# Attention values product in column halves, and block means from the loaded values: a change to a fused attention and two-MLP kernel

## The chip, the cores and the metric

The kernel runs on one core of a Trainium2 chip. The metric is the device time of one execution in microseconds (us), the median of several runs. The engines are TensorE (PE; its weight loads are shown apart as PEld), VectorE (DVE), ScalarE (ACT), GpSimd (POOL) and SyncE (SP), whose queue issues the DMA transfers here.

## The reference, cut to what matters

Two batches, 8 heads, 768 positions, head width 64, all float32. Each query attends to the keys less than 16 positions away and to 24 block summaries (block of 32 positions): the summary key is the block's maximum, the summary value its mean. The result goes through a gated MLP with an RMS norm and a second MLP.

```python
k_sum = k.reshape(B, H, nb, block, D).max(axis=3)
v_sum = v.reshape(B, H, nb, block, D).mean(axis=3)
scores_l_m = np.where(mask_l, scale * np.matmul(q, k.T), -1e9)
scores_s = scale * np.einsum('bhsd,bhnd->bhsn', q, k_sum) + np.log(block)
a = softmax(concatenate([scores_l_m, scores_s]))
v_all = np.concatenate([v, v_sum], axis=2)
x = np.matmul(a, v_all)                 # (1536, 512) after the heads are joined
xn = x / rms(x) * rms_g
x = (silu(xn @ w_gate) * (xn @ w_val)) @ w_out      # 512 -> 1536 -> 512
out = (s * relu(x @ w_in) ** 2 + b) @ w_out2        # 512 -> 2048 -> 512
```

## The kernel before

The 1536 rows (2 batches of 768) are 12 tiles of 128 queries. A tile is two halves of 64 queries; each half has its own window of 96 keys and the 24 summaries, so 120 keys in all (`KW` = 96, `KC` = 120). Heads go in two groups of four, so there are 24 groups of (tile, four heads).

For each group: `do_qk` (L587) multiplies queries and keys, four float32 matmuls; `do_top` (L597, DVE) adds the mask and finds the row maximum; `do_exp` (L604, ACT) takes the exponential and its sum; `do_t` (L615, PE) transposes the probabilities; `do_pt` (L634, ACT) copies the transposes out of PSUM; `do_pv` (L643, PE) is the values product; `do_norm` (L652, DVE) divides by the sum. A float32 matmul of the program shows as two MATMUL records in the trace.

The values product before: for each head one matmul, stationary the 120x128 transposed probabilities, moving the values of both halves beside one another (2 x 64 columns). All 128 queries are multiplied with the values of both windows, so half of what lands in PSUM is not wanted. `do_norm` is called twice for a group, once for each half: 64 partitions x 256 elements each.

The values lie in SBUF as slots of 96 window rows x 512 columns, one for each half tile (`vslot`), loaded by `load_v` (L282, six transfers of 384 KB for a batch). The 24 means stand in rows 96 to 119 of each slot. Before the change the means come from a second, transposed copy of v: `load_vt` (L322 and L327, four transfers of 384 KB for a batch, those of batch 1 into the ring of weight buffers `raw`), `sum_vt` (L332, one DVE reduction for each), `turn_vs` (L339, ACT, two small copies), `mean_vt` (L345, two PE transposes), `put_v` (L352 on DVE, L354 on ACT, scaling by 1/32 into a slot), and `spread_v` (L357), which copies the means by DMA from the slots that have them to the others.

From the six tiles on, the MLPs follow. Their weights are split in a high and a low part (DVE, ACT, POOL), and products run as float32r matmuls of 128x512 (L789, L790, L793, then L912, L913, L915). The first chunks of the first MLP (`HEAD` = 3, for three groups of 512 rows) are mixed with the attention as fill.

The order of the work up to there is made by a planner written out in the kernel: `plan` makes tasks with an engine, a cost, dependencies and a rank, and `give_out` (L373) issues, on a modelled clock, on each engine the task of lowest rank that could start. The result is a fixed program order for each engine, and each engine works through it in order. When TensorE would be idle in the plan, `give_out` issues four transposes of the identity matrix (L459), whose result nothing uses. SP's queue, too, is in a fixed order, and an issue that must wait holds those behind it.

Of the kernel before, what the change touches and what calls it, by code (L numbers as in the profile page):

```python
# [30 lines left out]
GH = 4  # L31
# [25 lines left out]
@with_exitstack  # L57
def kernel(ctx: ExitStack, tc: tile.TileContext, q_t, k_t, v_w, v_t, w_gate, w_val, w_out, w_in2, w_out2, rms_g, s2, b2, out):
    nc = tc.nc
# [41 lines left out]
    def bank(i):  # L101
        return psp.tile([128, 512], F32, tag=f"b{i}", name=f"b{i}")
# [9 lines left out]
    junk = const.tile([128, DM], mybir.dt.bfloat16, name="junk")  # L112
    qz = [const.tile([128, 2, GH, 128], F32, name=f"qz{i}") for i in range(2)]
    part = const.tile([128, NSUB * 4 * SUB], F32, name="part")

# [14 lines left out]
    def vslot(b, s):  # L130
        return vst[b][s // NTL][:, s % NTL]
# [18 lines left out]
    def consts_mask2():  # L150
        m, far = masks[1], masks[0]
        nc.gpsimd.tensor_copy(m[64:128, 0:KW], far[64:128, 0:KW])
        nc.gpsimd.memset(m[:, KW:KC], math.log(BLK) / scale)
        for i, p0, o in ((0, 0, HQ), (2, 64, HQ + WIN)):
            nc.gpsimd.tensor_copy(masks[i], m)
            nc.gpsimd.memset(masks[i][p0:p0 + 64, o:o + WIN], NEG / scale)

    def load_small():
# [149 lines left out]
    mean_ps = {}  # L308
    vt_t = {}
    vs_t = {}  # L310

    def vs_of(b):
        if b == 0:
            return vt0[:, NPAIR * SEQ:NPAIR * SEQ + 512]
        if b not in vs_t:
            vs_t[b] = tmp("vs")
        return vs_t[b]

    def load_vt(b, pr):
        if b == 0:  # L320
            t = vt_t[b, pr] = vt0[:, pr * SEQ:(pr + 1) * SEQ]
            nc.sync.dma_start(out=t, in_=v_t[b, pr])  # L322
            return
        t = rawp.tile([128, 512, 2], I32, tag="raw", name="vt")
        t = t.rearrange("p f c -> p (f c)")[:, 0:SEQ]
        vt_t[b, pr] = t.bitcast(F32)
        nc.sync.dma_start(out=t, in_=v_t[b, pr].bitcast(I32))  # L327

    def sum_vt(b, pr):

        c0 = pr * 128 + KW
        nc.vector.tensor_reduce(out=vs_of(b)[:, c0:c0 + NS].rearrange("p (c e t) -> p t c e", c=2, e=2),  # L332
                                in_=vt_t.pop((b, pr)).rearrange("p (t c e i) -> p t c e i", c=2, e=2, i=BLK), axis=AX.X, op=ALU.add)

    def turn_vs(b, pairs):

        vs = vs_of(b).rearrange("p (a c) -> p a c", a=NPAIR)[:, pairs]
        for o, a in ((64, KW + 12), (76, KW)):
            nc.scalar.activation(out=vs[:, :, o:o + 12], in_=vs[:, :, a:a + 12], func=AF.Copy)  # L339

    def mean_vt(b, pairs, i):
        vs = vs_of(b).rearrange("p (a c) -> p a c", a=NPAIR)[:, pairs]
        ps = mean_ps[b, pairs.start] = bank(i)
        for j in range(pairs.stop - pairs.start):
            nc.tensor.transpose(ps[:, j * 128:(j + 1) * 128], vs[:, j], ident)  # L345

    def put_v(b, s, pairs, eng):
        p0 = 64 if s % 2 else KW
        o = vslot(b, s)[KW:KC, pairs.start * 128:pairs.stop * 128]
        a = mean_ps[b, pairs.start][p0:p0 + NS, 0:(pairs.stop - pairs.start) * 128]  # L350
        if eng == "DVE":
            nc.vector.tensor_scalar(out=o, in0=a, scalar1=1.0 / BLK, scalar2=None, op0=ALU.mult)  # L352
        else:
            nc.scalar.activation(out=o, in_=a, func=AF.Copy, scale=1.0 / BLK)  # L354
# [116 lines left out]
    def mb(b):  # L471
        return b / 0.31e6

    def plan(x):
# [3 lines left out]
        cm2 = task("POOL", 1.4, consts_mask2, [cm], rank=-29.5)  # L478
        K, Q, V, VT, KM, VM = {}, {}, {}, {}, {}, {}

# [14 lines left out]

        def lvt(b, pr, rank):
            VT[b, pr] = task("SP", mb(128 * 768 * 4), lambda: load_vt(b, pr), rank=rank, take=("raw",) if b else ())

        def lv(b, t, rank):
# [6 lines left out]
        lq(1, (-6, -2.8))  # L506
        lvt(0, 0, -5)
        lvt(0, 1, -4.5)
        lv(0, 0, -4.2)
        lk(0, 4, -4)  # L510
        lk(0, 6, -3)
        lvt(0, 2, -2)
        lvt(0, 3, -1)
        for t in range(1, NTL):
            lv(0, t, t - 1.5)
        sml = task("SP", mb(128 * 516 * 4), load_small, rank=1.2)
        for h in range(0, NH, 2):
            lk(1, h, 4 + 0.5 * h)
        for pr in range(NPAIR):
            lvt(1, pr, 5.5 + pr)  # L520
        for t in range(NTL):
            lv(1, t, 9 + t)

# [19 lines left out]
        def means(b, rank):  # L543
            z = task("POOL", pl(512) / 3, lambda: nc.gpsimd.memset(vs_of(b), 0.0), rank=rank - 2 if b else -28)
            for g in range(2):
                pairs = slice(2 * g, 2 * g + 2)
                sums = [task("DVE", dve(768), lambda pr=pr: sum_vt(b, pr), [VT[b, pr], z], rank + 1.5 * g,
                             give=(("raw", VT[b, pr]),) if b else ()) for pr in (2 * g, 2 * g + 1)]
                tv = task("ACT", 0.54, lambda pairs=pairs: turn_vs(b, pairs), sums, rank + 1.5 * g)
                tr = task("PE", 0.22, lambda i, pairs=pairs: mean_vt(b, pairs, i), [tv, ci], rank + 1.5 * g, bank="M")  # L550
                VM[b, g] = tr
                puts = []
                for s in range(4 if b == 0 else 2):
                    e = ("ACT", "DVE")[s % 2]
                    puts.append(task(e, act(256) if e == "ACT" else dve(256), lambda s=s, e=e, pairs=pairs: put_v(b, s, pairs, e),
                                     [tr, *puts[-1:]] if s < 3 else [tr, puts[-1]], rank + 1.5 * g + s // 2))
                puts[-1]["free"] = (tr,)
                VM[b, g, "put"] = puts
            for t in range(NTL):
                if b == 0 and t < 2:  # L560
                    VM[b, t, "ok"] = [VM[b, g, "put"][2 * t + k] for g in range(2) for k in range(2)]
                elif b and t == 0:
                    VM[b, t, "ok"] = [p for g in range(2) for p in VM[b, g, "put"]]
                else:
                    first = [p for g in range(2) for p in VM[b, g, "put"]]
                    VM[b, t, "ok"] = [task("SP", 0.3, lambda s=s: spread_v(b, s), first, 2 * (6 * b + t) - 6) for s in (2 * t, 2 * t + 1)]
        means(0, -3.0)
# [8 lines left out]
        for n, (i, g) in enumerate(us):  # L576
# [60 lines left out]
            def do_pv(bk, i=i, g=g, b=b, t=t):  # L637
# [3 lines left out]
                for j in range(GH):  # L641
                    h = GH * g + j
                    nc.tensor.matmul(X[:, j * 128:(j + 1) * 128].rearrange("p (c d) -> p c d", c=2), PT[0:KC, j * 128:(j + 1) * 128],  # L643
                                     vv[:, :, h * HD:(h + 1) * HD], start=True, stop=True)
            C = pv[i, g] = task("PE", 0.88, do_pv, [pt, V[b, t], *VM[b, t, "ok"]], n + 0.2, bank="X", give=(("PT", pt),))

            def do_norm(c, i=i, g=g):
                if i not in X_of:
                    X_of[i] = xnp.tile([128, DM], F32, tag="xn", name="xn")
                p = slice(64 * c, 64 * c + 64)  # L650
                xv = box["X", i, g].rearrange("p (h c d) -> p h c d", h=GH, c=2)
                nc.vector.tensor_tensor(out=X_of[i][p, g * GH * HD:(g + 1) * GH * HD].rearrange("p (h d) -> p h d", h=GH),  # L652
                                        in0=xv[p, :, c],
                                        in1=sm_of[i][p, 1, GH * g:GH * g + GH].rearrange("p (h o) -> p h o", o=1).broadcast_to([64, GH, HD]),
                                        op=ALU.mult)
            N = [task("DVE", dve(256), lambda c=c, f=do_norm: f(c), [C, rc], n + 0.0) for c in range(2)]
            N[1]["deps"].append(N[0])
            N[1]["free"] = (C,)
            if g:
                N[0]["deps"].append(box["N", i][1])  # L660
                A["deps"].append(qk[i, 0])
# [6 lines left out]
            N = N + box["N", i]  # L668
            N[1]["give"] = (("sm", box["A0", i]),)

# [20 lines left out]
            if i == TPS:  # L691
                deps += [VM[0, 0], VM[0, 1]]
            if i == 2 * TPS:
# [249 lines left out]
def _layout(q, k, v, moe_w_gate, moe_w_val, moe_w_out, moe_rms_g, moe2_w_in, moe2_w_out, moe2_s, moe2_b):  # L943
# [26 lines left out]
    def strips(w):  # L970
# [5 lines left out]
        "v_w": c(vw),  # L976
        "v_t": c(v.reshape(NB, NPAIR, 2, SEQ, HD).transpose(0, 1, 2, 4, 3)).reshape(NB, NPAIR, 128, SEQ),
        "w_gate": c(strips(moe_w_gate)).reshape(KF, 128, 512),
# [30 lines left out]
```

## Time and profile before

| | us |
|---|---|
| median of 3 runs | 658.63 (654.58 to 660.88) |
| span of the profiled execution | 658.8 |
| PE busy in it | 634.1 (96%) |
| DVE busy | 396.6 (60%) |
| ACT busy | 269.8 (41%) |
| POOL busy | 153.8 (23%) |

The profile shows one execution. Busy time of PE is modelled, since matmuls are pipelined: where it is below the length of a stretch, TensorE waited at least that long. The span runs from the first to the last instruction; the page gives nothing of what lies around it, so 658.8 us is taken as this execution's own time.

### The profile page before, as it was taken

What the parts mean: (1) busy time and instruction counts of PE and PEld (TensorE: products, weight loads), DVE (VectorE), ACT (ScalarE), POOL (GpSimd) and SP (SyncE); (2) the same over time, 40 slices, a digit from 0 to 9 for tenths busy, and PEclk for the clock granted to TensorE, in tenths of its full rate; (3) what the DMA queues carried; (4) which work ended last, traced back from release to release, by engine and by line L of the source; (5) the groups of instructions that cost most, each with busy time, mean ns of one, the idle gap of its engine ahead of it and who ended that gap; (6) DMA issues with size and microseconds to landing.
All of it is one profiled execution on the core that took longest, in us unless ns stands there. A gap on an engine that the chain in (4) does not pass through costs nothing.

```text
span 658.8 us, 8381 instructions
## 1 busy us (share of the span) xinstructions
PE 634.1 (96%) x3052; PEld 529.9 (80%) x3052; DVE 396.6 (60%) x778; ACT 269.8 (41%) x615; POOL 153.8 (23%) x187
## 2 busy tenths in 40 slices
PE   4878989999999999999999999999999999999998
PEld 3777778888888888888888888888888888888886
DVE  5769999524681455554555666881278647855632
ACT  3765878332453333311333325552455035404400
POOL 3345756340331111111111111110221022102100
PEclk9989999999999999999999999999999999999999
DMA  9989951100342111111211111122021301120022
GB/s 290 266 248 269 276 160 66 33 0 14 115 135 89 59 66 67 64 66 64 65 64 65 64 60 42 61 66 93 1 96 65 97 32 65 64 65 0 1 96 97
DMA packets 20929, 59.36 MB, mean 90 GB/s; under 512 B 2664, under 2 KB 2920, under 8 KB 20888
## 3 DMA queue, kind: packets, MB, share of 16 engines
q1 hardware_dynamic: 20888, 58.83, 28.6%
q8 instruction: 24, 0.39, 0.3%
q14 instruction: 17, 0.14, 0.1%
HBM read 54.79 MB, written 3.15 MB: 88 GB/s over the span
## 4 chain that ended last, share of the span: by engine, by line
PE 86%; DVE 5%; DMA 4%; ACT 2%; SPq 1%; issue 1%; POOL 0%; DVEq 0%; ACTq 0%; POOLq 0%
PE b L793 21%; PE b L789 21%; PE b L790 21%; PE b L913 7%; PE b L915 7%; PE b L912 7%; DMA qz<-in_q_t_dram 3%; PE b L587 1%; ACT P L604 1%; SPq L357 1%; DMA hg<-in_k_t_dram 1%; PE b L643 1%; DVE ks L292 1%; DVE xn L652 1%; DVE wa L219 1%
## 5 line engine op out<-in xcount | busy, mean ns | idle before, releaser
L235 POOL TENSOR_TENSOR wl<-wa,wh 128x512 fp32r<-128x512 f32 x68 | 89.5, 1323 | 388.2 <-ACT wh L231 315.0
L789 PE MATMUL b<-x,wh 128*128 128x512 f32 x288 | 113.5, 394 | 0.3
L790 PE MATMUL b<-x,wl 128*128 128x512 f32 x288 | 112.3, 390 | 0.4 <-POOL wl L235 0.4
L231 ACT ACTIVATE wh<-wa 128x512 fp32r<-128x512 f32 x68 | 41.5, 626 | 98.8 <-PE b L915 45.5
L793 PE MATMUL b<-x,wh 128*128 128x512 f32 x288 | 77.6, 391 | 0.0
L913 PE MATMUL b<-wl,hg 128*128 128x512 f32 (+1 forms) x196 | 75.1, 385 | 0.0
L912 PE MATMUL b<-wh,hg 128*128 128x512 f32 (+1 forms) x196 | 75.1, 385 | 0.0
L789 PE MATMUL b<-y,wh 128*128 128x512 f32 x192 | 74.7, 389 | 0.0
L790 PE MATMUL b<-y,wl 128*128 128x512 f32 x192 | 74.7, 389 | 0.0
L894 DVE SCALAR_TENSOR_TENSOR b<-u,sbc 128x512 f32<-128x512 f32 x48 | 50.7, 1056 | 35.6 <-ACT u L893 35.6
L790 PEld LDWEIGHTS b<-x,wl 128*128 128x128 f32 x288 | 54.1, 188 | 11.4 <-POOL wl L235 0.7
L789 PEld LDWEIGHTS b<-x,wh 128*128 128x128 f32 x288 | 54.2, 188 | 11.3 <-issue 0.7
L793 PEld LDWEIGHTS b<-x,wh 128*128 128x128 f32 x288 | 53.6, 188 | 10.8
L789 PE MATMUL b<-hg,wh 128*128 128x512 f32 x144 | 56.0, 389 | 0.0
L790 PE MATMUL b<-hg,wl 128*128 128x512 f32 x144 | 56.0, 389 | 0.0
L814 DVE SCALAR_TENSOR_TENSOR hg<-b,bbc,hg 128x512 fp32r<-128x512 f32 x48 | 36.0, 749 | 28.2 <-ACT hg L813 28.2
L220 DVE SCALAR_TENSOR_TENSOR wa<-raw,wa 128x512 int32<-128x512 int32 x68 | 50.5, 743 | 2.1
L915 PE MATMUL b<-wh,hg 128*128 128x512 f32 (+1 forms) x196 | 51.5, 385 | 0.0
L793 PE MATMUL b<-y,wh 128*128 128x512 f32 x192 | 51.3, 389 | 0.0
L219 DVE SCALAR_TENSOR_TENSOR wa<-raw,wa 128x512 int32<-128x512 int32 x68 | 49.9, 734 | 2.1
L813 ACT ACTIVATE hg<-b,bbc 128x512 fp32r<-128x512 f32 x48 | 33.0, 687 | 42.9 <-DVE b L894 42.9
L921 DVE TENSOR_TENSOR part<-b,part 128x512 f32<-128x512 f32 (+1 forms) x37 | 24.4, 673 | 43.4 <-PE b L915 43.4
(94 smaller groups left out, 1010.3 us busy)
## 6 DMA issues: line engine op xcount, KB each, us to landing
raw<-in_w_out_dram SPq DMA_DIRECT2D x28, 512.0 KB
raw<-in_w_in_dram SPq DMA_DIRECT2D x16, 512.0 KB
qz<-in_q_t_dram SPq DMA_DIRECT2D x24, 256.0 KB
raw<-in_w_gate_dram SPq DMA_DIRECT2D x12, 512.0 KB
raw<-in_w_val_dram SPq DMA_DIRECT2D x12, 512.0 KB
vt<-in_v_t_dram SPq DMA_DIRECT2D x8, 384.0 KB
hg<-in_k_t_dram SPq DMA_DIRECT2D x5, 576.0 KB
out_dram<-part SPq DMA_DIRECT2D x11, 256.0 KB
```

Source lines behind the costliest of these rows:

```text
L219: lambda: nc.vector.scalar_tensor_tensor(out=ai, in0=hi, scalar=-0x80000000, in1=ai, op0=ALU.bitwise_and, op1=ALU.bitwise_or),
L220: lambda: nc.vector.scalar_tensor_tensor(out=ai, in0=lo, scalar=29, in1=ai, op0=ALU.logical_shift_right, op1=ALU.bitwise_or),
L231: nc.scalar.activation(out=r(h), in_=a_t[i], func=AF.Copy)
L235: nc.gpsimd.tensor_tensor(out=r(lo), in0=a_t.pop(i), in1=high[i], op=ALU.subtract)
L789: nc.tensor.matmul(ps, r(hi[:, kk * 128:(kk + 1) * 128]), xh, start=kk == 0, stop=False)
L790: nc.tensor.matmul(ps, r(lo[:, kk * 128:(kk + 1) * 128]), xh, start=False, stop=False)
L793: nc.tensor.matmul(ps, r(hi[:, kk * 128:(kk + 1) * 128]), r(act(kk, 1)), start=False, stop=kk == 3)
L814: nc.vector.scalar_tensor_tensor(out=r(dst[1]), in0=ps, scalar=bias, in1=dst[0], op0=ALU.add, op1=ALU.subtract)
L894: after(0, lambda u=u, ps=ps: nc.vector.scalar_tensor_tensor(out=ps, in0=u, scalar=sbc[:, 0:1], in1=u, op0=ALU.mult, op1=ALU.mult))
L912: nc.tensor.matmul(acc, gh, r(ws[e][0][:, cs]), start=e == 0, stop=False)
L913: nc.tensor.matmul(acc, gh, r(ws[e][1][:, cs]), start=False, stop=False)
L915: nc.tensor.matmul(acc, r(ge[e][:, 1]), r(ws[e][0][:, cs]), start=False, stop=e == 3)
```

## The change

The values product is made in two column halves: for each head two matmuls, one for each half of 64 queries, with 64 stationary columns and 64 moving columns, writing PSUM partitions 0 to 63 and 64 to 127. All 256 columns that land are wanted, and one `do_norm` of 128 partitions x 256 serves the group.

The block means are made from the loaded value slots. `sel` is a selection matrix of 0 and 1: `add_v` makes, for each of a batch's 12 slots, one float32 matmul of 64x32 by 64x512, which adds the two blocks of the slot into two of 32 PSUM rows; slots go by turns to the four strips of 32 partitions. `sums_v` copies the PSUM bank out (ACT), `mean_v` adds the four strips with one matmul (`comb`), and `put_v` writes 24x512 into a slot. The transposed copy of v is neither made on the host nor loaded. Ranks of the loads change: the six value loads of batch 0 come ahead of the queries of tile 2. The DMA scratch is made smaller.

```diff
+    def consts_sel():                      # POOL, 3 memsets
+        nc.gpsimd.memset(sel[0:64], 0.0)
+        nc.gpsimd.memset(sel[0:32, 17:18], 1.0)
+        nc.gpsimd.memset(sel[32:64, 23:24], 1.0)
+    def consts_comb():                     # POOL, 1 memset and 12 copies
+        nc.gpsimd.memset(comb, 0.0)
+        for j in range(4):
+            p = slice(32 * j, 32 * j + 32)
+            for o, a, n in ((KW, 0, 24), (64, 12, 12), (76, 0, 12)):
+                nc.gpsimd.tensor_copy(comb[p, o:o + n], ident[p, 32 * j + a:32 * j + a + n])
-    def load_vt(b, pr): ...
-    def sum_vt(b, pr): ...
-    def turn_vs(b, pairs): ...
-    def mean_vt(b, pairs, i): ...
+    def add_v(b, a, i):
+        if a == 0:
+            mean_ps[b] = bank(i)
+        for s in range(4 * a, 4 * a + 4):
+            j = s % 4
+            n0 = 12 * (s % 2) + s // 2
+            nc.tensor.matmul(mean_ps[b][32 * j:32 * j + 32], sel[0:64, 17 - n0:49 - n0], vslot(b, s)[0:64], start=a == 0, stop=a == 2)
+    def sums_v(b):
+        nc.scalar.activation(out=vs_of(b), in_=mean_ps[b], func=AF.Copy)
+    def mean_v(b, i):
+        ps = mean_ps[b] = bank(i)
+        nc.tensor.matmul(ps[0:KC], comb[:, 0:KC], vs_of(b), start=True, stop=True)
-    def put_v(b, s, pairs, eng):           # 24 x 256
+    def put_v(b, s, eng):                  # 24 x 512
-        lvt(0, 0, -5)
-        lvt(0, 1, -4.5)
-        lv(0, 0, -4.2)
+        lv(0, 0, -5)
+        lv(0, 1, -4.5)
-        lvt(0, 2, -2)
-        lvt(0, 3, -1)
-        for t in range(1, NTL):
-            lv(0, t, t - 1.5)
+        for t in range(2, NTL):
+            lv(0, t, -2.7 + 0.1 * t)
-        for pr in range(NPAIR):
-            lvt(1, pr, 5.5 + pr)
         for t in range(NTL):
-            lv(1, t, 9 + t)
+            lv(1, t, 6 + 0.6 * t)
+            for a in range(3):
+                add.append(task("PE", 0.9, lambda *i, a=a: add_v(b, a, *i or (None,)), [V[b, 2 * a], V[b, 2 * a + 1], cs, *add[-1:]],
+                                rank, bank="M" if a == 0 else None))
+            cp = task("ACT", act(512), lambda: sums_v(b), add[2:], rank, free=(add[0],))
+            tr = task("PE", 0.88, lambda i: mean_v(b, i), [cp, cc], rank, bank="M")
-                    nc.tensor.matmul(X[:, j * 128:(j + 1) * 128].rearrange("p (c d) -> p c d", c=2), PT[0:KC, j * 128:(j + 1) * 128],
-                                     vv[:, :, h * HD:(h + 1) * HD], start=True, stop=True)
+                    for c in range(2):
+                        nc.tensor.matmul(X[64 * c:64 * c + 64, j * HD:(j + 1) * HD], PT[0:KC, j * 128 + 64 * c:j * 128 + 64 * c + 64],
+                                         vv[:, c, h * HD:(h + 1) * HD], start=True, stop=True)
-            N = [task("DVE", dve(256), lambda c=c, f=do_norm: f(c), [C, rc], n + 0.0) for c in range(2)]
+            N = [task("DVE", dve(256), do_norm, [C, rc], n + 0.0, free=(C,))]
```

## Rows read from the trace of the kernel before

**Rows 1.** Busy time of each engine in four stretches: us, busy (instructions), clock, DMA share, GB/s

```profile
20.00:36.00 16.00, 11.46 (x94) 10.39 (x93) 10.39 (x47) 11.42 (x47) 6.61 (x13) 1.00 0.92 213
36.00:84.00 48.00, 44.08 (x305) 38.69 (x305) 42.57 (x150) 35.36 (x127) 27.64 (x43) 0.96 0.93 274
84.00:96.00 12.00, 9.34 (x82) 8.88 (x80) 11.66 (x25) 8.61 (x23) 7.86 (x8) 1.00 0.47 135
96.00:122.00 26.00, 24.98 (x165) 21.57 (x164) 24.59 (x79) 20.27 (x72) 14.61 (x23) 1.00 0.26 90
```

**Rows 2.** Chain of work that ended last: start us, us, what

```profile
15.43 9.68 DMA qz<-in_q_t_dram
25.17 10.46 DMA qz<-in_q_t_dram
...
47.78 0.42 DVE xn L652
...
57.22 0.86 DVE vs L332
...
72.23 0.43 DVE xn L652
...
80.97 0.88 DVE vs L332
...
92.00 3.35 DMA raw<-in_w_val_dram
...
101.01 0.89 PE b L643 x8
```

**Rows 3.** Timeline of the DMA issues on SP's queue, 80 to 95 us

```profile
83.80 8.09 SPq L357 DMA_DIRECT2D part<-part  x10
```

**Rows 4.** DMA view of the first 36 us: packets, bytes, mean rate; an issue group

```profile
DMA packets 4327, 9.37 MB, mean 260 GB/s; under 512 B 757, under 2 KB 757, under 8 KB 4323
...
vt<-in_v_t_dram SPq DMA_DIRECT2D x4, 384.0 KB
```

**Rows 5.** DVE groups by line, 0 to 122 us: busy us, mean ns

```profile
L652 DVE TENSOR_TENSOR xn<-b,sm 64x256 f32<-64x256 f32 x48 | 20.1, 419 | 2.1 <-PE b L643 0.9 <-POOL ss L679 0.3
...
L704 DVE TENSOR_TENSOR x<-b,x 128x512 fp32r<-128x512 f32 x11 | 7.5, 686 | 1.4 <-ACT x L702 1.3
...
L332 DVE TENSOR_REDUCE vs<-vt 128x24 f32<-128x768 f32 x4 | 3.8, 950 | 0.0
...
L352 DVE TENSOR_SCALAR hg<-b 24x256 f32<-24x256 f32 x4 | 1.7, 423 | 0.4 <-ACT hg L354 0.3
```

**Rows 6.** ACT groups by line, 0 to 122 us

```profile
L634 ACT ACTIVATE PT<-b 120x512 f32<-120x512 f32 x24 | 13.8, 589 | 0.9 <-PE b L615 0.6
...
L339 ACT ACTIVATE vs<-vs 128x24 f32<-128x24 f32 x4 | 0.7, 216 | 0.8 <-DVE vs L332 0.8
```

**Rows 7.** POOL timeline of the start

```profile
6.28 0.53 POOL L544 MEMSET vs<- 128x512 f32 x1
```

**Rows 8.** PE groups by line and shape, 0 to 140 us

```profile
L643 PE MATMUL b<-part,PT 120*128 120x128 f32 x96 | 12.2, 277 | 0.4 <-ACT PT L634 0.4
...
L459 PE MATMUL b<-ident 128*128 128x128 f32 x56 | 9.6, 299 | 0.3
```

**Rows 9.** PE timeline: the fifth values product, the last before 36 us

```profile
30.12 1.06 PE L643 MATMUL b<-hg,PT 120*128 120x128 f32 x8
```

**Rows 10.** PE timeline where the last MLP's half-width matmuls stand

```profile
652.46 0.28 PE L912 MATMUL b<-wh,hg 128*128 128x256 f32 x1
652.58 0.28 PE L913 MATMUL b<-wl,hg 128*128 128x256 f32 x1
```

**Rows 11.** PE timeline where float32 transposes change to float32r matmuls

```profile
59.01 0.48 PE L789 MATMUL b<-x,wh 128*128 128x512 f32 x1
59.33 0.39 PE L790 MATMUL b<-x,wl 128*128 128x512 f32 x1
59.56 0.40 PE L789 MATMUL b<-x,wh 128*128 128x512 f32 x1
```

More of the change, by code (lines that the diff above doesn't have):

```diff
@@ L57, with kernel @@
 @with_exitstack
-def kernel(ctx: ExitStack, tc: tile.TileContext, q_t, k_t, v_w, v_t, w_gate, w_val, w_out, w_in2, w_out2, rms_g, s2, b2, out):
+def kernel(ctx: ExitStack, tc: tile.TileContext, q_t, k_t, v_w, w_gate, w_val, w_out, w_in2, w_out2, rms_g, s2, b2, out):
     nc = tc.nc
@@ L113 @@
     qz = [const.tile([128, 2, GH, 128], F32, name=f"qz{i}") for i in range(2)]
+    sel = const.tile([128, 64], F32, name="sel")
+    comb = const.tile([128, 128], F32, name="comb")
     part = const.tile([128, NSUB * 4 * SUB], F32, name="part")
@@ L308 @@
     mean_ps = {}
-    vt_t = {}
     vs_t = {}
@@ L313, in vs_of @@
         if b == 0:
-            return vt0[:, NPAIR * SEQ:NPAIR * SEQ + 512]
+            return vt0[:, 0:512]
         if b not in vs_t:
@@ L317, in vs_of @@
         return vs_t[b]
[L319 to L345, printed above, removed]
-    def put_v(b, s, pairs, eng):
+    def add_v(b, a, i):
[11 more added lines that the diff above has]
+    def put_v(b, s, eng):
         p0 = 64 if s % 2 else KW
-        o = vslot(b, s)[KW:KC, pairs.start * 128:pairs.stop * 128]
-        a = mean_ps[b, pairs.start][p0:p0 + NS, 0:(pairs.stop - pairs.start) * 128]
+        o = vslot(b, s)[KW:KC]
+        a = mean_ps[b][p0:p0 + NS]
         if eng == "DVE":
@@ L478, in plan @@
         cm2 = task("POOL", 1.4, consts_mask2, [cm], rank=-29.5)
-        K, Q, V, VT, KM, VM = {}, {}, {}, {}, {}, {}
+        cs = task("POOL", 0.4, consts_sel, rank=-28)
+        cc = task("POOL", 2.5, consts_comb, [ci], rank=-27)
+        K, Q, V, KM, VM = {}, {}, {}, {}, {}
         def lk(b, h, rank, n=2):
@@ L494, in lq @@
                     Q[i, g] = task("ACT", 0.1, lambda g=g: load_qg(i, g, nc.scalar), deps[g:g + 1], rank=rank[g] - 3, more=QLAT)
-        def lvt(b, pr, rank):
-            VT[b, pr] = task("SP", mb(128 * 768 * 4), lambda: load_vt(b, pr), rank=rank, take=("raw",) if b else ())
         def lv(b, t, rank):
@@ L543, in means @@
         def means(b, rank):
[L544 to L558, printed above, removed]
+            add = []
@@ new lines, in means @@
+            for a in range(3):
[3 more added lines that the diff above has]
+            tr = task("PE", 0.88, lambda i: mean_v(b, i), [cp, cc], rank, bank="M")
+            VM[b] = tr
+            puts = []
+            for s in range(4 if b == 0 else 2):
+                e = ("ACT", "DVE")[s % 2]
+                puts.append(task(e, act(512) if e == "ACT" else dve(512), lambda s=s, e=e: put_v(b, s, e),
+                                 [tr, *puts[-1:]], rank + s // 2))
@@ L559, in means @@
+            puts[-1]["free"] = (tr,)
             for t in range(NTL):
                 if b == 0 and t < 2:
-                    VM[b, t, "ok"] = [VM[b, g, "put"][2 * t + k] for g in range(2) for k in range(2)]
+                    VM[b, t, "ok"] = puts[2 * t:2 * t + 2]
                 elif b and t == 0:
-                    VM[b, t, "ok"] = [p for g in range(2) for p in VM[b, g, "put"]]
+                    VM[b, t, "ok"] = puts
                 else:
-                    first = [p for g in range(2) for p in VM[b, g, "put"]]
@@ L566, in means @@
-                    VM[b, t, "ok"] = [task("SP", 0.3, lambda s=s: spread_v(b, s), first, 2 * (6 * b + t) - 6) for s in (2 * t, 2 * t + 1)]
+                    VM[b, t, "ok"] = [task("SP", 0.3, lambda s=s: spread_v(b, s), puts, 2 * (6 * b + t) - 6) for s in (2 * t, 2 * t + 1)]
         means(0, -3.0)
@@ L642, in do_pv, with do_norm @@
                     h = GH * g + j
-                    nc.tensor.matmul(X[:, j * 128:(j + 1) * 128].rearrange("p (c d) -> p c d", c=2), PT[0:KC, j * 128:(j + 1) * 128],
-                                     vv[:, :, h * HD:(h + 1) * HD], start=True, stop=True)
+                    for c in range(2):
+                        nc.tensor.matmul(X[64 * c:64 * c + 64, j * HD:(j + 1) * HD], PT[0:KC, j * 128 + 64 * c:j * 128 + 64 * c + 64],
+                                         vv[:, c, h * HD:(h + 1) * HD], start=True, stop=True)
             C = pv[i, g] = task("PE", 0.88, do_pv, [pt, V[b, t], *VM[b, t, "ok"]], n + 0.2, bank="X", give=(("PT", pt),))
-            def do_norm(c, i=i, g=g):
+            def do_norm(i=i, g=g):
                 if i not in X_of:
                     X_of[i] = xnp.tile([128, DM], F32, tag="xn", name="xn")
[L650 to L654, printed above, removed]
+                nc.vector.tensor_tensor(out=X_of[i][:, g * GH * HD:(g + 1) * GH * HD].rearrange("p (h d) -> p h d", h=GH),
+                                        in0=box["X", i, g][:, 0:GH * HD].rearrange("p (h d) -> p h d", h=GH),
+                                        in1=sm_of[i][:, 1, GH * g:GH * g + GH].rearrange("p (h o) -> p h o", o=1).broadcast_to([128, GH, HD]),
                                         op=ALU.mult)
-            N = [task("DVE", dve(256), lambda c=c, f=do_norm: f(c), [C, rc], n + 0.0) for c in range(2)]
-            N[1]["deps"].append(N[0])
-            N[1]["free"] = (C,)
+            N = [task("DVE", dve(256), do_norm, [C, rc], n + 0.0, free=(C,))]
             if g:
-                N[0]["deps"].append(box["N", i][1])
+                N[0]["deps"].append(box["N", i][0])
                 A["deps"].append(qk[i, 0])
@@ L668, in plan @@
             N = N + box["N", i]
-            N[1]["give"] = (("sm", box["A0", i]),)
+            N[0]["give"] = (("sm", box["A0", i]),)
             def do_rms(i=i):
@@ L691, in plan @@
             if i == TPS:
-                deps += [VM[0, 0], VM[0, 1]]
+                deps += [VM[0]]
             if i == 2 * TPS:
@@ L976, in _layout @@
         "v_w": c(vw),
-        "v_t": c(v.reshape(NB, NPAIR, 2, SEQ, HD).transpose(0, 1, 2, 4, 3)).reshape(NB, NPAIR, 128, SEQ),
         "w_gate": c(strips(moe_w_gate)).reshape(KF, 128, 512),
@@ L994 @@
     from concourse.bass_utils import run_bass_kernel_spmd as _run
-    nc = _bacc.Bacc("TRN2", target_bir_lowering=False, num_devices=1)
+    nc = _bacc.Bacc("TRN2", target_bir_lowering=False, num_devices=1, dynamic_dma_scratch_size=1024)
     arrays, args = {}, []
```

## The prediction

> **What bounds the kernel now.** I read the stretches first [rows 1], then the chain [rows 2], then groups by line. From 122 us on TensorE runs MLP matmuls without a gap, so nothing that the change touches can shorten that part; the end moves only as the attention ahead of it moves. Between 20 and 36 us TensorE is busy 11.46 of 16 us, and the chain is two query transfers of 9.68 and 10.46 us one behind the other [rows 2]: what they wait for is the DMA queue, which moved 9.37 MB in 36 us [rows 4]. Between 36 and 84 us DVE (42.57 of 48) and TensorE (44.08) are both near full, and the chain runs through DVE, reductions and normalisations among it [rows 2]. From 84 to 96 us TensorE is busy 9.34 of 12: ten copies of the means hold SP's queue for 8.09 us [rows 3], and the weight load behind them lands 3.35 us after its issue at 92.00 [rows 2]. From 96 to 122 us TensorE is busy 24.98 of 26: there only less TensorE work helps.
>
> The sum is made against this execution's 658.8 us; the median of the runs, 658.63, is 0.2 below, so it carries over as it is.
>
> **The change part by part.**
>
> *Early transfers.* Four transfers of 384 KB [rows 4] go (1.57 MB), but the last value load, which came behind the query load of the second chain row, now comes ahead: 0.39 MB. At 0.26 MB a us [rows 4] that query lands (1.57 - 0.39)/0.26 = 4.5 us earlier. Against it stands the first values product. It waited for four transposed loads and one value load; now for all six value loads: 0.39 MB more, 1.5 us. Behind them came a reduction of 0.95, two turns of 0.22, two transposes of 0.11 and two puts of 0.42 [rows 5, 6]: about 2.4 us. Now come one add call (0.89, below), a copy of 0.59 (the nearest is L634's), a matmul of 0.89, and two puts of 24x512 at 0.59 and 0.69 (nearest L634 and L704): 3.7 us. So it starts 2.8 us later. I take 4.5 - 2.8 = 1.7 us gained; bounds 4.5 gained (tiles 2 and 3 fill the wait) and 2.8 lost.
>
> *DVE.* 24 normalisations of 0.42 us go, since one over 128 partitions has the same 256 elements each (the same 0.42 by that row), and eight reductions of 0.95 [rows 5]: 10.1 + 7.6 = 17.7 us less. Six puts of 0.42 become three of 0.69. Only what lies on the chain counts at once. There, three of batch 1's reductions stand with 0.86 to 0.88 us each, and the fourth at 80.97 (the first and the last of the four stand in rows 2): 3.5 us; nine pieces of L652 from 47.78 to 72.23, 3.4 us in all [rows 2], of which half goes: 1.7. Together 5.2 us. Next late is TensorE: in 36 to 84 us it has 48 - 44.08 = 3.9 us free [rows 1], and 28 of the 56 identity transposes of L459 [rows 8] stand there, at the pitch of 0.11 us below 3.1 us: 7.0 us that can be closed. Batch 1's means add to it 3 x 0.89 + 0.89 - 4 transposes x 0.11 = 3.1 us. So 5.2 + 3.1 - 7.0 = 1.3 us doesn't fit, and 3.9 us is gained. Bounds: 0, and 9.4 (all four reductions and the half of some 26 normalisations there).
>
> *The copies of the means.* All 18 `spread_v` transfers stay. Batch 1's no longer wait for transposed loads that take `raw` buffers, so their 8 us of SP come earlier, over a deeper queue of transfers. TensorE's shortfall in 84 to 96 us is 2.7 us [rows 1]; I take half, 1.3; bounds 0 and 2.7.
>
> *TensorE, values product.* A group's eight records take 0.89 us [rows 2], 0.111 each. Halving both operands' columns gives 16 records. No row has 64 columns. The nearest pair is the last MLP's: at 512 columns 0.23 between starts [rows 11], at 256 0.12 [rows 10], so the pitch goes nearly with the columns. I take 0.056 a record, 0.89 a group, no change. Bounds: 0.111 a record as if the columns didn't count (1.78 a group), and two halves at once (0.45).
>
> *TensorE, the adds.* A float32 matmul of 512 columns is two records of 4 x 0.111, 0.89 us. Four of `add_v` write four different strips of 32 partitions. No row has strips. If they run at once a call is 0.89, if one after the other 3.55. I take 0.89, since 32 of 128 columns of the array are used by each; both ends stay in the range. Batch 0's first two calls stand between 10 and 20 us where the identity transposes fill idle TensorE [rows 8]; the third is in the chain above.
>
> The Trainium skill ("TensorE: Matmul & The Clock Gate", Measured speedup vs the span model) gives 2.38 times for three column strips. By it four of them would take an estimated 1.1 us a call. No row here shows it.
>
> *POOL and the rest.* Two memsets of 0.53 go [rows 7]; four memsets and twelve copies of 64 columns or less come; at 0.53 each, the price of 512 columns, 8.5 us at most. POOL is otherwise done at 6.8 us, and they are needed at the first add and at `mean_v`, the latter behind 20 us: nothing. On ACT six puts of 24x256 and eight turns become three puts of 24x512 and two copies of 128x512, some 3 us in all, and in 36 to 84 us ACT is idle 48 - 35.36 = 12.6 us [rows 1]: nothing.
>
> Sum: 1.7 + 3.9 + 1.3 = 6.9 us, 658.8 - 6.9 = 651.9, said as 652.
>
> **The rivals.**
>
> *Halves of the product overlap* (two strips of 64 columns at once): 0.89 - 0.45 = 0.44 us less in each of the 19 groups behind 36 us (five stand before it [rows 9]), where TensorE is near full: 8.4 us more gained, 644. For it: the same reason as for the adds. Against: then two instructions would have to start within each 0.03 us, and no row starts records closer than 0.11.
>
> *Changes of kind cost.* From the transposes to the next float32r matmul the first start-to-start gap is 0.32 instead of 0.23 [rows 11]: 0.09. If going into and out of halves costs that each, 2 x 19 x 0.09 = 3.4 us, 655. The Trainium skill ("TensorEngine Tiling (Array Packing)", Key Properties) says that a change of the tiling mode drains TensorE. A drain by rows is a record's 0.277 less its pitch of 0.111 [rows 2, 8], 0.17: 2 x 19 x 0.17 = 6.3, 658. So this case spans 655 to 658.
>
> *The strips run one after the other.* A call is 3.55, 2.66 more. Batch 1: 3 x 2.66 = 8.0 on a full TensorE. Batch 0: the last call delays the first product by 2.66, the others go in idle time. 10.6 us, 662.5: the gain and some more is gone. For it: each call's matmuls are two records on one strip, which must follow one another, and TensorE takes its records in order; if only the second record overlaps the next strip's first, a call is 5 x 0.444 = 2.2, half of the extra price, 657.
>
> *Slower: the record, not the column, has the price.* The place is `do_pv`, 16 records for 8. At 0.111 each a group is 0.89 longer, 19 groups 16.9 us, 652 + 16.9 = 669. It decides from 0.056 + 6.9/(19 x 16) = 0.079 us a record: above that the whole gain is gone. For it: no record in the trace starts sooner than 0.11 behind another, whatever its shape. Against: 512 to 256 columns shows only 0.013 us that doesn't go with columns.
>
> **How the numbers follow.** A measurement of this kernel can't tell less than about 1% (its three runs span 6.3 us), so faster means below 652.0 and slower above 665.2. The forecast (646 to 657, the errors of its three terms) 0.46, half of it on either side of 652; the halves overlap (640 to 648) 0.14, faster; changes of kind 0.14, of which 0.03 faster, the rest same; serial strips (656 to 667) 0.13, 0.08 same and 0.05 slower; price by record (660 to 675) 0.13, 0.02 same and 0.11 slower. Faster 0.40, same 0.44, slower 0.16. The range goes from 641 to 666, which leaves out about 0.05 below and 0.12 above.
>
> **What would show it.** Right: a group's 16 records of `do_pv` in 0.9 us; L652 24 times at 0.42; `add_v` calls of about 0.9 us; the query load that landed at 35.6 us landing by 32; TensorE's stretch of pure MLP starting some 7 us sooner. Wrong: start-to-start gaps of 0.08 or more in `do_pv`, `add_v` calls of 2 us or more with the transposes behind them late, first `do_pv` behind 28 us, or TensorE still waiting for DVE in what was 36 to 84 us. The sum is wrong as a whole if the new order of the planner puts a record that waits for a value load ahead of ready work, since TensorE takes no other meanwhile.

## The result and the profile after

The changed kernel takes 651.32 us, the median of 18 runs (650.21 to 654.27), against 657.21 us (653.45 to 660.88, 18 runs) for the kernel before: a ratio of 0.9915, 95% interval 0.9897 to 0.9932, so 0.85% faster. The forecast was 652.0, within 641 to 666, with a change within 1% as the likeliest outcome.

The two profiled executions are 658.8 and 648.9 us long, 9.9 apart, where the medians are 5.9 apart. The one of before was a long one for its kernel: device time lies 1.8 us above the span (650.68 for the span of 648.9), which puts it near 660.6. TensorE fell to a mean granted clock of 0.79 between 36 and 44 us in it, behind a wait of 3.3 us for queries. Only a part of the executions show this. Of 57 runs of the kernel before beside the experiments, 46 have a mean clock of 0.999 or more over the whole run and a median of 656.2 us; the other 11 have 0.994 to 0.997 and take 657.4 to 661.9. Of the changed kernel's 18 runs one has less than 0.999. So most of the 4 us between 9.9 and 5.9 belong to this execution, and where neither clock falls the change gains some 5 us (656.2 to 651.2).

Busy time of the engines in the same four stretches, after (us, then PE, PEld, DVE, ACT, POOL with their instructions, granted clock, DMA share, GB/s):

```profile
20.00:36.00 16.00, 14.72 (x154) 10.92 (x153) 9.49 (x47) 12.36 (x44) 4.58 (x8) 1.00 0.91 300
36.00:84.00 48.00, 44.02 (x462) 35.17 (x461) 42.78 (x169) 43.21 (x156) 37.44 (x55) 1.00 0.78 250
84.00:96.00 12.00, 10.91 (x123) 9.11 (x122) 9.79 (x40) 11.10 (x43) 8.87 (x11) 1.00 0.29 100
96.00:122.00 26.00, 26.00 (x167) 21.23 (x166) 10.34 (x24) 10.77 (x29) 9.66 (x13) 1.00 0.00 1
```

Beside [rows 1]: between 36 and 84 us DVE is as busy as before (42.78 against 42.57), though each group asks less of it, and ACT goes from 35.36 to 43.21. More groups pass through the same 48 us: TensorE starts 13 values products in it instead of 9. Between 96 and 122 us DVE is down from 24.59 to 10.34: the attention is over sooner. When it ends is shown by the transposes of the last tile into the MLP's layout, before

```profile
122.51 0.60 PE L689 MATMUL b<-ident,xn 128*128 128x128 f32 x4
```

and after, here with the first values product, a group of it alone, two groups in a row, a call of `add_v`, and `mean_v` (start us, us, engine, line):

```profile
26.54 1.04 PE L347 MATMUL b<-vt,comb 128*120 128x512 f32 x2
...
28.66 0.33 PE L637 MATMUL b<-hg,PT 120*64 120x64 f32 x2 [0.20 <-ACT hg L356]
...
45.40 0.69 PE L637 MATMUL b<-hg,PT 120*64 120x64 f32 x16 [0.68 <-ACT PT L627]
46.02 0.66 PE L679 MATMUL b<-ident,xn 128*128 128x128 f32 x4
...
47.49 1.06 PE L340 MATMUL b<-part,sel 64*32 64x512 f32 x8
48.49 0.70 PE L608 MATMUL b<-ident,P 128*120 128x128 f32 x4
...
53.52 1.17 PE L637 MATMUL b<-hg,PT 120*64 120x64 f32 x32 [0.25 <-ACT PT L627]
54.61 1.26 PE L340 MATMUL b<-part,sel 64*32 64x512 f32 x8
...
108.09 0.60 PE L679 MATMUL b<-ident,xn 128*128 128x128 f32 x4
```

A group of 16 records takes 0.62 us from its start to that of the next work (45.40 to 46.02), not 0.89; two groups in a row take 1.09 (53.52 to 54.61), 0.55 each. An add call takes 1.00 us (47.49 to 48.49). The last transposes start at 108.1 instead of 122.5, 14.4 us sooner; the time gained is less, since only 80 of the MLP's matmuls stand ahead of them now, against 100 before. The other 20, at 0.23 us each, follow later: 14.4 - 4.6 = 9.8 us, the difference of the two executions.

The two lines of DVE that answer to [rows 5]:

```profile
L644 DVE TENSOR_TENSOR xn<-b,sm 128x256 f32<-128x256 f32 x24 | 10.0, 420 | 1.2 <-PE b L637 1.1
...
L354 DVE TENSOR_SCALAR hg<-b 24x512 f32<-24x512 f32 x2 | 1.4, 690 | 1.2 <-ACT hg L356 1.2
```

And the chain of work that ended last, some of its longest pieces, beside [rows 2]:

```profile
41.86 7.63 DMA qz<-in_q_t_dram
...
74.82 4.63 DMA raw<-in_w_val_dram
...
81.40 2.08 ACT P L597 x11
...
87.84 2.06 ACT P L597 x11
```

Where DVE's pieces filled the chain from 47 to 76 us before, TensorE's do up to 62 us now, and mostly ACT's from there to 92 us. The ten copies of batch 1's means stand on SP's queue from 65.88 us instead of 83.80 [rows 3], and the weight load behind them is still waited for (74.82, 4.63 us).

### The profile page after: what moved, and what is told of

Same layout as the page of the kernel before. It is cut to its first block, busy times and chain, and to the rows that moved or that the text cites. A ratio compares the mean times of both kernels' runs of the same rounds, so it can differ in the third digit from the quotient of the medians.

```text
span 648.9 us, 8741 instructions
## 1 busy us (share of the span) xinstructions
PE 630.3 (97%) x3260; PEld 518.3 (80%) x3260; DVE 373.3 (58%) x743; ACT 267.4 (41%) x606; POOL 156.4 (24%) x201
## 4 chain that ended last, share of the span: by engine, by line
PE 90%; ACT 4%; DMA 3%; DVE 1%; issue 1%; POOL 0%; SPq 0%; ACTq 0%; DVEq 0%; POOLq 0%
PE b L783 22%; PE b L779 21%; PE b L780 21%; PE b L903 7%; PE b L905 7%; PE b L902 7%; ACT P L597 2%; PE b L580 1%; DMA qz<-in_q_t_dram 1%; PE b L637 1%; PE b L608 1%; DMA hg<-in_k_t_dram 1%; PE b L340 1%; DMA raw<-in_w_val_dram 1%; PE b L679 1%
## 5 line engine op out<-in xcount | busy, mean ns | idle before, releaser
L235 DVE SCALAR_TENSOR_TENSOR wa<-raw,wa 128x512 int32<-128x512 int32 x68 | 50.0, 735 | 2.0
L234 DVE SCALAR_TENSOR_TENSOR wa<-raw,wa 128x512 int32<-128x512 int32 x68 | 48.7, 717 | 2.0
```

Source lines behind the costliest of these rows:

```text
L234: lambda: nc.vector.scalar_tensor_tensor(out=ai, in0=hi, scalar=-0x80000000, in1=ai, op0=ALU.bitwise_and, op1=ALU.bitwise_or),
L235: lambda: nc.vector.scalar_tensor_tensor(out=ai, in0=lo, scalar=29, in1=ai, op0=ALU.logical_shift_right, op1=ALU.bitwise_or),
```

## The experiments

All times are medians, and the diffs are cut to what matters. The kernel before, run beside each of three sets of experiments, took 656.25, 656.32 and 656.96 us; the ratio and its 95% interval are against these. After the trace was read, two theories stood against each other. W: the gain is waits taken away, at the DMA queue and on DVE, since TensorE's own work comes out even (24 x 0.27 = 6.5 us less in the products, 6 x 1.0 + 2 x 0.88 - 8 x 0.11 = 6.9 us more for the means). P: the gain is TensorE's shorter products, and the means only cost. A kernel whose plan changes gets another order of instructions throughout; the experiments that keep the changed kernel's order are marked so, and their times stand against 651.32 (and 651.94, a second measurement of it beside the last set).

**Halves alone.** The product in halves and one normalisation on the kernel before; means as before.

```diff
+ for c in range(2): matmul(X[64*c:64*c+64, ...], PT[0:KC, j*128+64*c : ...+64], vv[:, c, ...])
+ one do_norm of 128 x 256 for a group
  means: load_vt, sum_vt, turn_vs, mean_vt as before
```

> The values product in halves with one normalisation, the block means as before. Theory W (the gain is waits taken away: 3 MB less on the DMA queue, 18 us less on DVE; TensorE's own work comes out even): DVE loses 10 of the 18 us and TensorE 6.7 us here, no transfer goes; about half of the 5.9 us, 653 to 655. Rival P (the gain is TensorE's: a group of the values product takes 0.61 instead of 0.89 us, 24 x 0.28 = 6.7 us, and the means only add work): all of it and more, since the means' 7.1 us of adds on TensorE aren't paid: 646 to 650.

649.38 us, 0.9886 (0.9849 to 0.9924): at least the whole change's gain. So far this is P's number.

**Means alone.** The other half of the diff, product and normalisation as before.

```diff
- for c in range(2): matmul(X[64*c:64*c+64, ...], ...)
+ matmul(X[:, j*128:(j+1)*128], PT[0:KC, j*128:(j+1)*128], vv[:, :, ...])
+ do_norm twice, 64 x 256
```

> The block means from the loaded values, the values product as before. Theory W: 3 MB and 7.6 us of DVE go, TensorE gets 7.1 us, most of it at times when it waits: 653 to 656. Rival P: TensorE has 7.1 us more and nothing less, so slower than before, 659 to 664.

659.34 us, 1.0036 (1.0015 to 1.0057): a little slower than before. P again. A part of it may be the clock: eight of the ten runs have a mean clock of 0.997, and the two at 1.000 took 657.66 and 658.89. The stretches show what W had missed:

```profile
36.00:84.00 48.00, 42.42 (x302) 34.52 (x301) 41.16 (x143) 35.58 (x123) 31.08 (x46) 0.96 0.75 222
84.00:96.00 12.00, 12.00 (x93) 11.18 (x92) 10.46 (x51) 11.47 (x42) 6.14 (x12) 1.00 0.24 72
96.00:122.00 26.00, 26.00 (x173) 23.14 (x172) 20.88 (x62) 16.68 (x59) 12.98 (x21) 1.00 0.18 62
```

From 84 us on TensorE has no free time at all (12.00 and 26.00), where before it had 2.7 and 1.0 [rows 1]: what the means freed elsewhere, TensorE gave back in its own added work.

**Two normalisations again.** Same order as the changed kernel.

```diff
- tensor_tensor(X_of[:, ...], X[:, 0:256], sums of 128)
+ for c in range(2): p = slice(64*c, 64*c+64); tensor_tensor(X_of[p, ...], X[p, 0:256], sums[p])
```

> The changed kernel with its instructions in the same order, but the normalisation of a group in two instructions of 64 partitions, as before the change: 24 x 0.42 = 10.1 us more on DVE, TensorE as it is. Theory W: 2 to 5 us of it come back at the end, 653 to 656. Rival P, and the case that ACT alone bounds the attention now: 651 to 652, nothing.

655.64 us, 0.9986 (0.9969 to 1.0002): 4.3 us lost, most of the change's gain. DVE's lines show the one thing that differs:

```profile
L646 DVE TENSOR_TENSOR xn<-b,sm 64x256 f32<-64x256 f32 x48 | 20.1, 419 | 1.7 <-PE b L637 1.3
```

10.1 us more on DVE cost 4.3. P allowed nothing here; W had it right. TensorE's busy time in the whole execution, first of the changed kernel, then of this one, shows how:

```profile
PE 630.3 (97%) x3260; PEld 518.3 (80%) x3260; DVE 373.3 (58%) x743; ACT 267.4 (41%) x606; POOL 156.4 (24%) x201
```

```profile
PE 629.8 (96%) x3260; PEld 516.5 (79%) x3260; DVE 383.6 (59%) x767; ACT 268.3 (41%) x606; POOL 154.2 (24%) x201
```

Its work is the same; taken from the spans of 648.9 and 653.6 us, its free time goes from 18.6 to 23.8. The waits that grow are those of the products for ACT's copy of the probabilities (from 2.3 to 7.7 us between 20 and 110 us), though ACT has no more to do: a wait names the engine that came last, not the one whose work made it late.

**Heads inside, halves outside.** Same order but for the eight products of a group.

```diff
- for j in range(GH):
-     for c in range(2):
+ for c in range(2):
+     for j in range(GH):
```

> The changed kernel with the matmuls of a group of the values product in another order: all four heads of the first half, then all four of the second; nothing else moves. If the 0.61 us come from two halves at once, a group is 16 x 0.058 = 0.93 us, 0.3 longer, 24 x 0.3 = 7.7 us more on TensorE. Rival P: the gain is gone, 656 to 659. Theory W: part of it falls into waits, 653 to 656. If the 0.61 come from the halved columns alone, nothing moves: 651 to 652.

652.32 us, 0.9934 (0.9911 to 0.9958). Two lines of its timeline:

```profile
42.47 0.97 PE L637 MATMUL b<-hg,PT 120*64 120x64 f32 x16
43.37 0.65 PE L608 MATMUL b<-ident,P 128*120 128x128 f32 x4
```

A group takes 0.90 us now: the 0.62 come from halves running at once, which they do when neighbours in the program go to different halves of the array. TensorE's busy time over the whole execution goes from 630.3 to 635.4 us:

```profile
PE 635.4 (98%) x3260; PEld 523.9 (81%) x3260; DVE 373.2 (57%) x743; ACT 267.9 (41%) x606; POOL 155.9 (24%) x201
```

Of these 5.1 us the span shows 1.6 (650.5 against 648.9) and the medians 1.0, which the two intervals don't tell from nothing. The other 3.5 went into time that TensorE had free (15.1 us of it left, of 18.6). P falls with this, and W's 653 to 656 was too much as well. In the changed kernel the single normalisation is worth 4.3 us and the overlap about 1 when each is undone alone; both undone together were not tried.

**All adds in one strip.** Same order.

```diff
- matmul(mean_ps[b][32*j:32*j+32], sel, vslot(b, s)[0:64], start=a == 0, stop=a == 2)    # j = s % 4
+ matmul(mean_ps[b][0:32], sel, vslot(b, s)[0:64], start=s == 0, stop=s == 11)
```

> The changed kernel with all twelve add matmuls of a batch in one strip of 32 partitions (each slot has columns of its own there, so the sums are the same) instead of four by turns; the order is the same. If strips run at once, as the 0.99 us of a call say, one strip makes a call 3.5 us, six calls 15 us more on TensorE, of which batch 0's lie partly in idle time: 658 to 664. If TensorE were covered by the other engines in the attention: 652 to 654.

667.34 us, 1.015 (1.0106 to 1.0194), 16.0 us above the changed kernel and more than either case gave.

```profile
13.33 7.03 PE L339 MATMUL b<-hg,sel 64*32 64x512 f32 x8
...
26.82 3.62 PE L339 MATMUL b<-hg,sel 64*32 64x512 f32 x8
30.37 1.15 PE L579 MATMUL b<-kx,qz 128*128 128x120 f32 x8
```

A call takes 3.55 us (26.82 to 30.37), and the first, where TensorE has only just begun to work, 6.97 (13.33 to 20.30; in the changed kernel 1.86). Together the six calls take 5.1 + 5 x 2.55 = 17.9 us more, of which 16.0 show in the time. Four strips at once are what makes this way of taking means possible; one after the other it would have been the slower case.

**The transposed loads again.** Same order; nothing reads what they bring.

```diff
  nc.sync.dma_start(out=t, in_=v_w[b, :, s0:s0 + n])
+ if b == 0 and s0 < 8:
+     nc.sync.dma_start(out=vt0[:, 512 + pr*SEQ : ...], in_=v_t[b, pr])
```

> The changed kernel with the four transposed value loads of batch 0 (4 x 384 KB) issued again, each behind a value load; nothing reads them. If bytes on the DMA queue ahead of the first values product set the time, 1.6 MB at 0.3 MB a us are 5 us there: 654 to 656. If only the order of work on the engines counts: 651 to 652.

658.65 us, 1.0024 (1.0000 to 1.0047): 7.3 us for 1.57 MB, more than the 5 to 6 us that the queue's rate gives. The chain, and the stretch behind it:

```profile
16.28 12.06 DMA hg<-in_v_w_dram
```

```profile
28.00:36.00 8.00, 7.47 (x26) 4.43 (x27) 1.50 (x9) 3.03 (x11) 1.26 (x2) 0.57 1.03 365
```

The adds wait for the last value loads. Behind two such waits, of 0.9 and 0.5 us, TensorE's mean clock is 0.57 from 28 to 36 us: it runs at the lower of its two levels (1.2 GHz) for most of that time, among others the last adds and `mean_v`. That is 8 x 0.43 = 3.4 us of full clock lost, so the 7.3 are not the queue's alone. Nine of the ten runs have a mean clock of 0.992 to 0.995; the one at 1.000 took 656.07, 4.8 us above the changed kernel, which may be nearer to what the loads cost by themselves, though it is a single run.

**Batch 0's means as before, batch 1's by selection**, with the halves.

```diff
+ means0(0, -3.0)      # load_vt, sum_vt, turn_vs, mean_vt, put_v of 24 x 256
  means(1, M1)         # add_v, sums_v, mean_v
```

> The values product in halves; the block means of batch 0 as before the change (transposed loads), those of batch 1 by selection matmuls. Why do the means cost some 2 us on top of the halves? If it is the later first values product (28.7 instead of 24.5 us, since it waits for all six value loads), this kernel has the halves' gain and batch 1's saved transfers and reductions besides: 646 to 648.5. If it is the 7.1 us that the adds put on TensorE, it lies halfway between the halves alone (649.4) and the whole change (651.3): 650 to 651.

656.12 us, 0.9994 (0.9969 to 1.0020): neither theory's number, 6.7 us above the halves alone. Three stretches, first of the halves alone, then of this kernel:

```profile
28.00:36.00 8.00, 5.57 (x57) 5.21 (x58) 3.66 (x19) 5.42 (x24) 4.22 (x8) 1.00 0.76 204
...
60.00:84.00 24.00, 22.04 (x216) 19.06 (x216) 22.23 (x87) 21.50 (x80) 20.08 (x24) 1.00 0.84 226
84.00:122.00 38.00, 37.54 (x303) 30.65 (x301) 24.43 (x72) 23.60 (x75) 19.56 (x27) 1.00 0.30 98
```

```profile
28.00:36.00 8.00, 6.51 (x63) 5.85 (x63) 2.70 (x13) 6.30 (x25) 4.21 (x10) 0.79 0.83 218
...
60.00:84.00 24.00, 23.93 (x234) 18.77 (x234) 17.84 (x74) 20.22 (x70) 16.65 (x20) 1.00 0.73 216
84.00:122.00 38.00, 34.64 (x269) 28.00 (x269) 24.40 (x79) 23.72 (x79) 19.29 (x26) 0.96 0.24 80
```

TensorE is full from 60 to 84 us while DVE is fed less (17.84 against 22.23), and waits 3.4 us from 84 on. The clock falls twice, to a mean of 0.79 in 28 to 36 us, behind a wait of 1.2 us for queries, and to 0.96 in 84 to 122 us, behind one of 3.0 us for ACT's copy; the halves alone show 1.00 in both. By these rows 8 x 0.21 + 38 x 0.04 = 3.2 us of full clock are lost, an estimate of up to half of the 6.7. All ten runs have a mean clock of 0.992 to 0.997. The planner made another order out of other tasks; which task tipped it was not tried. It shows that a re-planned kernel can move by some 6 us through its order and the falls of the clock that come with it, so the halves alone and the means alone, too, price their parts only that closely.

**More work on ACT.** Same order.

```diff
  activation(PT[0:KC], T[0:KC], Copy)
+ activation(junk[0:KC, 0:320], T[0:KC, 0:320], Copy)
```

> The changed kernel with a second, smaller copy out of PSUM on ACT behind each copy of the transposed probabilities, into a buffer that nothing reads: 24 x 0.4 = some 10 us more on ACT, nothing else. The like of it on DVE (the normalisation in two parts) cost 4.3 us. If ACT is now what the attention waits for most, 5 to 9 us: 656 to 660. If DVE still is, less than 4: 652 to 655.

652.60 us, 0.9938 (0.9915 to 0.9961).

```profile
L628 ACT ACTIVATE junk<-b 120x320 bf16<-120x320 f32 x24 | 10.4, 434 | 0.0
```

10.4 us more on ACT cost 1.3, which the intervals don't tell from nothing, where 10.1 on DVE cost 4.3. The extra copy stands behind the one that the products wait for, so this is its price at that place. The chain after is full of ACT's pieces, and yet ACT is not what the attention waits for most.

**Without batch 0's last add call**, same order, and **without two of batch 1's**, same order.

```diff
+ if b == 0 and a == 2: return          # one kernel
+ if b == 1 and a: return               # the other
```

> The changed kernel, all in the same order, without the last of batch 0's three add calls: the blocks of its last four slots are missing in the means. The chain to the first values product then no longer waits for the last two value loads, and TensorE has 1 us less there. If the means' cost beside the halves is the late first values product, 1.5 to 3 us come back: 648.5 to 650. If it is the work on TensorE, 0.5 to 1: 650.5 to 651.

652.39 us, 0.9926 (0.9900 to 0.9953): no gain. But its first values product started at

```profile
28.07 0.33 PE L639 MATMUL b<-hg,PT 120*64 120x64 f32 x2 [0.22 <-ACT hg L358]
```

only 0.6 us sooner, since a query load took the last value loads' place as what TensorE waits for; and a second profile of the changed kernel has it at 26.86 us with nothing left out. It says little on the price of a late first product.

> The changed kernel, all in the same order, without the second and third of batch 1's add calls: the blocks of its last eight slots are missing in the means. TensorE has 2 us less at 47 to 62 us. If its work is what counts there, 1.5 to 2 us come back: 649.5 to 650. If TensorE waits for other engines there anyway, 0 to 0.5: 651 to 651.5.

649.80 us, 0.9882 (0.9842 to 0.9923): 1.5 to 2.1 us back for some 2 us of TensorE, as if little covered it. The interval reaches over that of the changed kernel, so this points at TensorE's work and doesn't settle it.

**The planner told 0.62 us for a group**, on the halves alone, and **the whole change once more**.

```diff
- C = task("PE", 0.88, do_pv, ...)
+ C = task("PE", 0.62, do_pv, ...)
```

> The halves alone, with the planner told the cost that the trace shows for a group of the values product, 0.62 instead of 0.88 us. If the order suffers from the wrong cost: 646 to 649. If it only changes the order by chance: 648 to 652, either way of the halves alone (649.4).

649.90 us, 0.9876 (0.9826 to 0.9925): as the halves alone.

> The changed kernel once more, beside the runs of this call: 651.3. The halves alone gave 649.4; if the means cost something of their own, this one stays 1 to 3 us above that.

651.94 us, 0.9927 (0.9892 to 0.9962). The halves alone (649.38) lie 1.9 to 2.6 us below the changed kernel's two medians, but the intervals overlap. Six of the eight runs of the two halves kernels are faster than the fastest of the changed kernel's 18 (650.21); that the halves alone beat the whole change is likely, not shown.

## Why the prediction was right

The total was right, 652.0 for 651.32, and its direction; the split behind it was not. Terms that were too large and too small made up for one another, so that it came this close is luck.

*The time of before.* The sum took 658.8 as the execution's own time. Device time is 1.8 us above the span, and that execution was a long one, so the base was a mixture that happened to lie near the median (657.21). That its clock was at 0.96 between 36 and 84 us stands in [rows 1] and got no term; where the clock doesn't fall the kernel takes 656.2, and the change gains some 5 us, not 6.9.

*Early transfers (1.7 gained).* The first values product was forecast 2.8 us later; it started at 28.66 instead of 24.51, 4.2 later, and 2.4 later (26.86) in the second profile of the same kernel. A start behind 28 us was named as a sign of being wrong; it was seen, and the total held all the same. The 4.2 us that TensorE waited for queries between 20 and 37 us are gone. What four such loads are worth was put at 1.57 MB / 0.26 = 6 us; the experiment gave 7.3 with a low clock in it and 4.8 in the run without. The mechanism holds and the size is of the right order; what the later product cost by itself was not separated.

*DVE (3.9 gained).* One normalisation of 128 partitions takes 0.42, as forecast. But I gave the normalisations 1.7 us of the gain and the reductions 3.5; undone, the normalisation alone costs 4.3, and the means, with their reductions gone, make the kernel 0.4% slower, the clock's part included. Reading the shares off the chain's pieces was the failing step: the chain names whichever engine came last at each point, and what a piece that repeats in each group costs when it grows was not to be read there.

*The copies of the means (1.3 gained).* They stand 18 us earlier, and TensorE in 84 to 96 us is busy 10.91 instead of 9.34, 1.6 more. About right, though the queue is still held for 7.7 us and a weight load still waited for.

*The values product (nothing).* Wrong by 0.27 a group. The rival of overlapping halves had the mechanism, and the argument against it (no record starts sooner than 0.11 behind another) took a pitch that goes with columns for a limit on starts. It was not true of the trace either: float32r matmuls (L789, L793) start some 0.03 us behind the record ahead of them where they follow one of another kind. Its price was far off: 8.4 us were forecast (for 19 groups; four stand before 36 us, not five, so 20 follow), and the order that takes the overlap away costs 1.0. The assumption that TensorE is near full there, so that each us of it counts, is what failed for products: 3.5 of 5.1 us went into its free time.

*Changes of kind.* The 0.09 were read from a gap behind the first float32r record; that record itself starts 0.03 us behind the last transpose, 0.08 sooner than the pitch, so the row shows next to no cost. Going into and out of halves does have one. In the trace the records of the two halves start in pairs, 0.058 us from pair to pair. Eight such steps would be 0.47 us a group; it takes 0.62 alone and 0.55 where two follow one another. So some 0.15 us goes into entering and leaving, once for two groups in a row, close to that rival's 2 x 0.09 by luck, and is paid out of the overlap. The Trainium skill ("TensorEngine Tiling (Array Packing)", Key Properties) says that a change of the tiling mode drains TensorE; the trace agrees in kind, and 0.15 for the pair is below the 2 x 0.17 of a full drain each way.

*The adds (0.89 a call).* 1.00 measured in four of the six calls (1.20 in the one at 54.61, 1.86 in the first), so four strips run at once. In the trace the first records of all four start within 0.02 us and the second ones 0.45 us later, so the rival's argument, that a strip's two records hold up the next strip, did not hold. The Trainium skill's figure for three strips ("TensorE: Matmul & The Clock Gate", Measured speedup vs the span model), from which 1.1 was estimated, is near it too. The rival of serial strips was priced at 10.6 us; the experiment gave 16.0 of the 17.9 us by which the calls grew: the forecast that batch 0's first two calls fall into idle time did not hold in this order.

*ACT and POOL (nothing).* POOL's new constants cost nothing visible. ACT's busy time in 36 to 84 us rose to 43.21, which "nothing" did not foresee, but 10.4 us more on it cost only 1.3.

*Price by the record.* Refuted: two records start for each 0.058 us, and 0.90 us for 16 records in the other order is 0.056 each.

What stays open is why the means cost what they do beside the halves, some 2 us in the medians. TensorE's account points at its work. The halves alone have

```profile
PE 624.9 (97%) x3232; PEld 517.6 (80%) x3232; DVE 383.0 (59%) x754; ACT 268.9 (42%) x615; POOL 155.9 (24%) x187
```

in a span of 647.2 us, so 22.3 free. In the changed kernel TensorE is busy 5.4 us longer and has 3.7 us less free time: the means took waits away, but fewer than they added. Two calls out gave 1.5 to 2.1 back, and alone the means fill TensorE from 84 us on. The late first product could not be taken away by itself, and the order that the planner makes is mixed into the comparison. The new ranks of the loads and the smaller DMA scratch were not tried by themselves; the halves alone have neither and keep the gain.

## What to carry to other kernels

A microsecond has a different price on each engine and at each place, and neither the busy shares nor the pieces of the chain gave it: here some 10 us more on DVE cost 4.3 and on ACT 1.3, 5.1 more in TensorE's products about 1, and 17.9 more in its adds 16.0. Undo one part at a time inside a fixed order to learn it, and add up the busy and the free time of the engine that bounds the kernel to see where it went. Work moved from a loaded engine to the one that bounds the kernel has to be paid there: the reductions freed DVE and the transfers freed the queue, and TensorE's adds took it back. A comparison of two plans mixes all this with the order, and before a wait is blamed, compare the granted clocks of the two executions.

## What the runs showed of the hardware

Float32 matmuls that write different 32-partition strips, or different halves, of PSUM ran at once: four of 64x32 by 64x512 in 1.00 us against 3.55 in one strip, two halves of 64 columns in 0.62 us a group against 0.90. The neighbours in the program had to go to different halves for it: the same 16 records in the other order lost most of it.

TensorE's clock fell to the lower of its two levels behind waits in some executions only: to a mean of 0.79 from 36 to 44 us in the profile before (behind 3.3 us), 0.57 from 28 to 36 us with the transposed loads again (behind 0.9 and 0.5 us), 0.79 from 28 to 36 us with batch 0's means as before (behind 1.2 us). Of the kernel before, runs at a clock of 0.999 or more took 656.2 us in the median, those below it 659.3.
